# Channel attention on one core: the row buffer starts 128 bytes earlier in SBUF

## The chip, the core and the metric

The kernel runs on one core of a Trainium2 chip. Its time is the device time of one execution in microseconds (us). Before the change it is 717.7 us, the median of 3 runs (717.59 to 718.36).

## What is computed

The input x is an image of 384 x 384 places with 384 channels in bf16, 113.25 MB. The mean of every channel over all places is multiplied by one weight (the kernel size k is 1, so the convolution over channels is a product), goes through a sigmoid, and scales its channel:

```
g = jnp.einsum("bhwc->bc", x) / (H * W)
s = sigmoid(g * w1d[0])            # the loop over k, with k = 1
return x * s[:, None, None, :]
```

All of x must have been read before the first output can be written, and x is larger than the core's on-chip memory (SBUF).

## The kernel before, in words

**Rows and partitions.** One row is the 384 channels of one place, 768 bytes. The 147,456 rows are spread over 128 partitions, 1,152 each. The first chunk of the image, 785 rows for each partition, is called STREAMED; the second, 367 rows for each partition, KEPT. A partition's rows of a chunk lie next to each other in HBM, so a transfer of n rows is, in each partition, one run of n x 768 bytes in HBM and one run in SBUF.

**The arena.** Nearly all of SBUF is one tile, `arena`, with 275 rows for each partition (211,200 bytes of it). Every load and every store of the image goes into or out of it; TensorE, VectorE, ScalarE and GpSimd read it, the last three write it. The tiles of the pool are laid out in the order of their declarations, each rounded up to a multiple of 32 bytes for each partition.

**First half, about 268 us.** SyncE's queue loads rows (`load`, L235, its DMA at L240). TensorE sums them with a matrix of ones into one PSUM bank (`sum_rows`, L257, its instructions recorded at L246). STREAMED rows are summed and overwritten. KEPT rows remain: VectorE folds four rows into the room of three (`fold`, L296, with the helpers at L280 and L286; ScalarE checks at L317 that the dropped exponent bits are the expected ones and leaves its findings in `seen`). Some rows are copied to the PSUM banks as well (L382). The table `PLAN` (L396) sets the order of loads, sums and folds.

**The turn.** ScalarE takes the sigmoid of the sums (L431), with the factor `w_sc` as its scale. `w_sc` comes from the weight, which was loaded to `w_bf`.

**Second half.** VectorE, and GpSimd beside it, multiply rows by the result (`scale`, L439, recorded at L444); VectorE unfolds the folded rows first (L491 on). SyncE's queue stores the rows (`store`, L465, its DMA at L471) and loads the 784 rows of STREAMED that are no longer there a second time. A loop (L724 on), run when the program is written, keeps a model of the DMA queue and so fixes the order of all these steps; nothing in it depends on addresses in SBUF. At the end `worst` (the largest entry of `seen`), `odd` and `odd_i` tell GpSimd whether any row had unexpected exponents, in which case rows would be done again; with this data none has.

**Waits.** `Flow` (L107 and L113 among its lines) writes each step out on its engine with the semaphores it needs. All of the image's transfers are on SyncE's one queue, in one order.

Of the kernel before, what the change touches and what calls it, by code (L numbers as in the profile page):

```python
# [131 lines left out]
def kernel(  # L132
# [12 lines left out]
    P = nc.NUM_PARTITIONS  # L145
    B, H, W, C = x.shape
# [5 lines left out]
    bf16, f32, u16, u32 = x.dtype, mybir.dt.float32, mybir.dt.uint16, mybir.dt.uint32  # L152
# [15 lines left out]
    ROWS = Y + 2 * PIECE  # L168
# [13 lines left out]
    pool = ctx.enter_context(tc.tile_pool(name="sb", bufs=1))  # L182
# [2 lines left out]
    pieces = [(g, lo, min(PIECE, q - lo)) for g, (_, q) in enumerate(GROUPS) for lo in range(0, q, PIECE)]  # L185

    ones = pool.tile([P, P], bf16, name="ones")
    w_bf = pool.tile([1, 1], bf16, name="w_bf")
    w_sc = pool.tile([P, 1], f32, name="w_sc")
    worst = pool.tile([P, 1], f32, name="worst")  # L190
    odd = pool.tile([P, 1], bf16, name="odd")
    arena = pool.tile([P, ROWS, C], bf16, name="arena")
    s_bf = pool.tile([P, C], bf16, name="s_bf")
    rest = pool.tile([P, P], bf16, name="rest")
    seen = pool.tile([P, 2 * len(pieces)], f32, name="seen")
# [664 lines left out]
```

## Time and profile before

| | |
|---|---|
| median of the runs | 717.7 us |
| the profiled execution | 717.85 us |
| its span, from the first to the last instruction | 715.6 us |
| transfers of the image on SyncE's queue | 63 loads, 48 stores |
| read from HBM, written | 190.32 MB, 113.25 MB |
| busiest engine | VectorE (DVE), 467.5 us |

The profile's page names the engines PE (TensorE), DVE (VectorE), ACT (ScalarE), POOL (GpSimd) and SP (SyncE); SPq is SyncE's queue. A group's row has the line in the kernel, the engine, the operation, output and input tile, shapes and count, then the busy time in us, the mean of one in ns, and the idle time before it with what ended it. A stage's row has the stretch and its length in us, then each engine's busy time with its count of instructions, the clock granted to TensorE, the share of the 16 DMA engines' time that their packets fill, and the rate in GB/s. A queue's row has packets, MB, and the share of the 16 engines' time. A packet is what one DMA engine moves as one piece: here one partition's run of one transfer, or a few bytes that report its end.

### The profile page before, as it was taken

What the parts mean: (1) busy time and instruction counts of PE and PEld (TensorE: products, weight loads), DVE (VectorE), ACT (ScalarE), POOL (GpSimd) and SP (SyncE); (2) the same over time, 40 slices, a digit from 0 to 9 for tenths busy, and PEclk for the clock granted to TensorE, in tenths of its full rate; (3) what the DMA queues carried; (4) which work ended last, traced back from release to release, by engine and by line L of the source; (5) the groups of instructions that cost most, each with busy time, mean ns of one, the idle gap of its engine ahead of it and who ended that gap; (6) DMA issues with size and microseconds to landing.
All of it is one profiled execution on the core that took longest, in us unless ns stands there. A gap on an engine that the chain in (4) does not pass through costs nothing.

```text
span 715.6 us, 2106 instructions
## 1 busy us (share of the span) xinstructions
PE 221.1 (31%) x1279; PEld 0.3 (0%) x3; DVE 467.5 (65%) x383; ACT 116.5 (16%) x97; POOL 98.0 (14%) x46
## 2 busy tenths in 40 slices
PE   4658877999998890000000000000000000000000
PEld 0000000000000000000000000000000000000000
DVE  4600001898989849999999999999940597007840
ACT  3700001576667630000110000000000000000000
POOL 0000000000000005414233431167100000000000
PEclk9899989999999996555555555555555555555555
DMA  9999999999999989999999999999999999999997
GB/s 382 428 446 419 439 431 425 447 422 433 425 430 427 430 351 379 407 418 435 427 428 437 441 422 437 443 435 430 444 414 459 423 431 442 420 435 439 442 426 326
DMA packets 15997, 303.70 MB, mean 424 GB/s; under 512 B 1778, under 2 KB 2418, under 8 KB 5106
## 3 DMA queue, kind: packets, MB, share of 16 engines
q1 hardware_dynamic: 15984, 303.57, 99.0%
q8 instruction: 5, 0.08, 0.0%
q14 instruction: 6, 0.05, 0.0%
q10 hardware_dynamic: 2, 0.00, 0.0%
HBM read 190.32 MB, written 113.25 MB: 424 GB/s over the span
## 4 chain that ended last, share of the span: by engine, by line
DMA 49%; DVE 29%; PE 16%; ACT 1%; issue 1%; DVEq 0%; SPq 0%; another core or an unknown queue 0%; POOLq 0%
DMA arena<-in_x_dram 37%; DVE arena L444 20%; PE bank L246 16%; DMA out_dram<-arena 11%; DVE arena L280 5%; DVE arena L286 4%; ACT arena L317 1%; DVEq L107 0%; SPq L471 0%; SPq L240 0%; ACT s_bf L431 0%; SPq L113 0%; SPq L855 0%; POOLq L107 0%
## 5 line engine op out<-in xcount | busy, mean ns | idle before, releaser
L246 PE MATMUL bank<-arena,ones 128*128 128x384 bf16 x1151 | 200.6, 337 | 37.5 <-DMA arena<-in_x_dram 37.5
L280 DVE TENSOR_SCALAR arena<-arena 128x1536 uint16<-128x1536 uint16 (+2 forms) x199 | 140.5, 751 | 107.1 <-DMA arena<-in_x_dram 100.0
L444 POOL TENSOR_TENSOR arena<-arena,s_bf 128x768 bf16<-128x768 bf16 (+3 forms) x42 | 97.8, 2333 | 426.5 <-ACT bank L435 268.1
L444 DVE TENSOR_TENSOR arena<-arena,bank 128x3072 bf16<-128x3072 bf16 (+13 forms) x61 | 138.0, 2303 | 4.4 <-DMA arena<-in_x_dram 3.7
L444 DVE TENSOR_TENSOR arena<-arena,s_bf 128x5376 bf16<-128x5376 bf16 (+4 forms) x27 | 76.5, 2902 | 94.9 <-DMA arena<-in_x_dram 84.8
L317 ACT ACTIVATE arena<-arena 128x3072 uint16<-128x3072 uint16 (+1 forms) x38 | 102.5, 2696 | 146.2 <-DVE arena L280 146.2
L286 DVE TENSOR_TENSOR arena<-arena 128x3072 uint16<-128x3072 uint16 (+2 forms) x90 | 117.7, 1307 | 12.2 <-PE bank L246 9.3
L561 PE MATMUL bank<-odd,ones 128*128 128x1 bf16 x1 | 0.2, 187 | 259.5 <-DVE odd L556 259.5
L246 PE MATMUL bank<-s_bf,ones 128*128 128x384 bf16 x125 | 22.1, 326 | 0.0
L382 ACT COPY arena<-bank 128x512 uint32<-128x512 uint32 (+2 forms) x8 | 4.2, 533 | 87.4 <-DMA out_dram<-arena 87.3
L317 ACT ACTIVATION_READ_ACCUMULATOR arena<-arena 128x1 f32 x38 | 7.1, 187 | 0.0
L382 ACT COPY bank<-arena 128x512 uint32<-128x512 uint32 (+2 forms) x8 | 3.8, 527 | 0.0
L260 PE MATMUL bank<-arena,ones 128*128 128x384 bf16 x1 | 0.5, 479 | 6.9 <-DMA arena<-in_x_dram 6.9
L431 ACT ACTIVATE s_bf<-bank,w_sc 128x384 bf16<-128x384 f32 x1 | 0.6, 580 | 9.4 <-PE bank L246 9.4
L828 ACT ACT_TABLE_LOAD x1 | 1.3, 1283 | 0.7 <-PEq L844 0.7
L337 DVE MEMSET ones<- 128x128 bf16 x1 | 0.2, 165 | 1.1 <-PEq L844 1.1
L342 PE MATMUL bank<-w_bf,ones 1*128 1x1 bf16 x1 | 0.2, 182 | 2.1 <-DMA w_bf<-in_w1d_dram 2.1
L347 DVE TENSOR_SCALAR w_sc<-bank 128x1 f32<-128x1 f32 x1 | 0.2, 159 | 0.9 <-PE bank L342 0.9
L565 DVE CAST odd_i<-bank 128x1 int32<-128x1 f32 x1 | 0.2, 157 | 0.3 <-PE bank L561 0.3
L561 PEld LDWEIGHTS bank<-odd,ones 128*128 128x128 bf16 x1 | 0.1, 105 | 517.6 <-DVE odd L556 517.6
L435 ACT COPY bank<-s_bf 128x192 uint32<-128x192 uint32 x1 | 0.3, 323 | 0.0
L382 ACT COPY arena<-rest 128x64 uint32<-128x64 uint32 x1 | 0.2, 244 | 0.0
(10 smaller groups left out, 1.4 us busy)
## 6 DMA issues: line engine op xcount, KB each, us to landing
arena<-in_x_dram SPq DMA_DIRECT2D x3, 6912.0 KB, 36.2
out_dram<-arena SPq DMA_DIRECT2D x3, 6912.0 KB, 28.4
arena<-in_x_dram SPq DMA_DIRECT2D x4, 4608.0 KB, 24.2
arena<-in_x_dram SPq DMA_DIRECT2D x6, 3072.0 KB, 19.8
out_dram<-arena SPq DMA_DIRECT2D x6, 3072.0 KB, 21.5
arena<-in_x_dram SPq DMA_DIRECT2D x2, 6144.0 KB, 30.7
arena<-in_x_dram SPq DMA_DIRECT2D x2, 4992.0 KB, 23.4
arena<-in_x_dram SPq DMA_DIRECT2D x1, 8160.0 KB, 26.5
```

Source lines behind the costliest of these rows:

```text
L246: return pe.add_instruction(mybir.InstMatmult(name=nc.get_next_instruction_name(), ins=[pe.lower_ap(rhs), pe.lower_ap(ones[:])], outs=[pe. ...
L260: return nc.tensor.matmul(acc, lhsT=ones[:], rhs=arena[:, i, :], start=first, stop=last)
L280: lambda: nc.vector.tensor_scalar(out=dst, in0=src, scalar1=s0, scalar2=s1, op0=op0, op1=op1),
L286: "DVE", lambda: nc.vector.tensor_tensor(out=dst, in0=a, in1=b, op=op), reads=reads, writes=writes
L317: lambda: nc.scalar.activation(out=y, in_=y, func=ACTF.Copy, accum_out=seen[:, 2 * k + i : 2 * k + i + 1]),
L337: fl.add("DVE", lambda: nc.vector.memset(ones[:], 1.0), writes=["ones"])
L382: "ACT", lambda: nc.scalar.copy(dst.bitcast(u32), src.bitcast(u32)), reads=reads, writes=writes
L431: lambda: nc.scalar.activation(out=s_bf[:], in_=acc, func=ACTF.Sigmoid, scale=w_sc[:, 0:1]),
L435: "ACT", lambda: nc.scalar.copy(s_ps.bitcast(u32), s_bf[:].bitcast(u32)), reads=["s_bf"], writes=["bank0"]
L444: lambda: vec.tensor_tensor(out=v, in0=v, in1=s[:, None, :].to_broadcast([P, n, C]), op=Op.mult),
L561: lambda: nc.tensor.matmul(votes, lhsT=ones[:], rhs=odd[:], start=True, stop=True),
L828: nc.scalar.preload_act_table(ACTF.Sigmoid)
```

## The change

The four small tiles `w_bf`, `w_sc`, `worst` and `odd` are declared behind the arena and no longer in front of it. Each takes 32 bytes of a partition. The pool begins at byte 16,512 of a partition with `ones`, 256 bytes.

| tile | first byte before | first byte after |
|---|---|---|
| `ones` | 16,512 | 16,512 |
| the four small tiles | 16,768 to 16,864 | 227,968 to 228,064 |
| `arena` | 16,896 = 66 x 256 | 16,768 = 65.5 x 256 |
| `s_bf` | 228,096 | 228,096 |

```diff
     ones = pool.tile([P, P], bf16, name="ones")
+    arena = pool.tile([P, ROWS, C], bf16, name="arena")
     w_bf = pool.tile([1, 1], bf16, name="w_bf")
     w_sc = pool.tile([P, 1], f32, name="w_sc")
     worst = pool.tile([P, 1], f32, name="worst")
     odd = pool.tile([P, 1], bf16, name="odd")
-    arena = pool.tile([P, ROWS, C], bf16, name="arena")
     s_bf = pool.tile([P, C], bf16, name="s_bf")
```

Every engine has the same instructions in the same order before and after, SyncE's transfers included. The lines of the kernel keep their numbers, apart from those of the five declarations.

## The prediction

> **What bounds the kernel now.** I read the page's totals first, then the stages, then the DMA queue's own packets.
>
> ```profile
> span 715.6 us, 2106 instructions
> PE 221.1 (31%) x1279; PEld 0.3 (0%) x3; DVE 467.5 (65%) x383; ACT 116.5 (16%) x97; POOL 98.0 (14%) x46
> DMA packets 15997, 303.70 MB, mean 424 GB/s; under 512 B 1778, under 2 KB 2418, under 8 KB 5106
> q1 hardware_dynamic: 15984, 303.57, 99.0%
> HBM read 190.32 MB, written 113.25 MB: 424 GB/s over the span
> ```
>
> No engine is busy for more than 65% of the span, but the packets of queue q1 fill 99.0% of the time of 16 DMA engines. The chain of waits names three parties, and it would mislead a reader who stopped there:
>
> ```profile
> DMA 49%; DVE 29%; PE 16%; ACT 1%; issue 1%; DVEq 0%; SPq 0%; another core or an unknown queue 0%; POOLq 0%
> ```
>
> It follows dependencies. A PE or DVE piece on it runs while the DMA engines still have earlier transfers queued. The table by stage shows this; its last two columns are the DMA share (1.00 means all 16 engines busy) and GB/s:
>
> ```profile
> 0.00:20.00 20.00, 8.89 (x42) 0.20 (x2) 10.17 (x18) 8.57 (x7) 0.20 (x4) 1.00 0.95 393
> 20.00:110.00 90.00, 64.76 (x352) 0.00 (x0) 9.42 (x16) 11.17 (x15) 0.00 (x0) 0.91 1.00 431
> 110.00:215.00 105.00, 99.84 (x600) 0.00 (x0) 79.83 (x109) 60.88 (x43) 0.00 (x0) 0.98 1.00 431
> 215.00:265.00 50.00, 44.96 (x272) 0.00 (x0) 39.17 (x53) 30.54 (x22) 0.00 (x0) 1.00 1.01 425
> 265.00:290.00 25.00, 2.46 (x16) 0.00 (x0) 21.71 (x18) 0.90 (x2) 9.21 (x3) 0.65 0.86 335
> 290.00:350.00 60.00, 0.00 (x0) 0.00 (x0) 57.36 (x33) 0.00 (x0) 21.49 (x10) 0.50 1.01 424
> 350.00:450.00 100.00, 0.00 (x0) 0.00 (x0) 97.34 (x64) 4.41 (x9) 35.03 (x12) 0.50 1.01 433
> 450.00:550.00 100.00, 0.19 (x1) 0.10 (x1) 76.33 (x53) 0.00 (x0) 32.12 (x18) 0.50 1.01 436
> 550.00:640.00 90.00, 0.00 (x0) 0.00 (x0) 39.27 (x13) 0.00 (x0) 0.00 (x0) 0.50 1.00 432
> 640.00:715.60 75.60, 0.00 (x0) 0.00 (x0) 36.87 (x13) 0.00 (x0) 0.00 (x0) 0.50 0.95 410
> ```
>
> Outside the start, the turn from reading to writing (265 to 290) and the tail, the DMA share is 1.00 or 1.01 (a packet that crosses a window's edge counts whole). So what is added to the packets is added to the time; where the engines idle, about 1.0 us at the start, 25 x 0.14 = 3.5 us at the turn and 75.6 x 0.05 = 3.8 us at the end, the idling is for the first bytes, the sigmoid and the last landing, which stay.
>
> **What a packet costs now.** A rate and a fixed price come out of two stretches that hold only loads, one of large packets and one of small:
>
> ```profile
> DMA packets 907, 38.77 MB, mean 431 GB/s; under 512 B 101, under 2 KB 101, under 8 KB 101
> q1 hardware_dynamic: 906, 38.76, 99.6%
> ...
> DMA packets 2650, 21.27 MB, mean 425 GB/s; under 512 B 294, under 2 KB 425, under 8 KB 1277
> q1 hardware_dynamic: 2648, 21.24, 100.5%
> ```
>
> The first pair is 20 to 110 us: 906 packets and 38.76 MB took 99.6% of 16 x 90 us = 1,434.2 us. The second is 215 to 265 us: 2,648 packets and 21.24 MB took 100.5% of 16 x 50 us = 804.0 us. With f for each packet and b for each MB, 906f + 38.76b = 1,434.2 and 2,648f + 21.24b = 804.0. Scaling the first by 21.24/38.76 and subtracting leaves 2,151f = 18.1 us, so f = 8.4 ns (about 0.5 ns either way from the rounding of the shares) and b = 36.81 us, which is 27.17 GB/s for one engine. Over the whole span this gives (15,984 x 0.0084 + 303.57 x 36.81)/16 = 706.8 us, where the page's 99.0% is 708.4: nothing large is missing. All 16 engines reach 434.7 GB/s, and the stages stand at 431 to 436.
>
> **The change part by part.** The order of instructions on every engine, and the size and shape of each, stay as they are, so nothing is removed, added or moved past a queue. Four tiles of 32 bytes come to stand behind the arena. The arena's first byte goes from 16,896 = 66 x 256 to 16,768 = 65.5 x 256, and since a row is 768 = 3 x 256 bytes, every row then starts 128 bytes past a multiple of 256. The tiles from s_bf on keep their addresses. The four small tiles are used by seven instructions in all; I cost these at nothing wherever the tiles lie. They run beside the full DMA queue; without that cover even a doubling of the longest of them would add 0.6 us:
>
> ```profile
> L431 ACT ACTIVATE s_bf<-bank,w_sc 128x384 bf16<-128x384 f32 x1 | 0.6, 580 | 9.4 <-PE bank L246 9.4
> L347 DVE TENSOR_SCALAR w_sc<-bank 128x1 f32<-128x1 f32 x1 | 0.2, 159 | 0.9 <-PE bank L342 0.9
> ```
>
> What is left is the arena's side of every transfer. Their number:
>
> ```profile
> L240 SPq DMA_DIRECT2D arena<-in_x_dram x63: 327/339/1270, 0.9 to 622.4; - x63
> L471 SPq DMA_DIRECT2D out_dram<-arena x48: 332/333/1268, 268.5 to 688.3; - x48
> ```
>
> 63 loads and 48 stores are 111 transfers of 128 partitions. Each sends one data packet per partition: 111 x 128 = 14,208, and with 16 small ones per transfer 111 x 144 = 15,984, the count of q1 exactly. One engine thus carries 888 data packets, 504 of loads and 384 of stores.
>
> The trace has no packet whose SBUF side starts off a multiple of 256, so the price is bounded. From below: nothing, if only the number of bytes counts. A gain would have to come out of the 8.4 ns, and I see no reason why a start off a boundary should shorten them. From above, within one packet: if SBUF is read and written in blocks of 256 bytes, a packet of n blocks that starts in the middle of one touches n + 1, a whole block more, 256 x 36.81e-6 us = 9.4 ns; this is close to paying the fixed price a second time. I take half of that, 128 bytes or 4.7 ns: the half block ahead of the first byte is carried for nothing, while the last block can stop at its last byte. It is the middle of the bounds, and the nearest row, the 8.4 ns, doesn't exclude either end.
>
> 888 x 4.7 ns = 4.2 us. The profiled execution took 717.85 us (715.6 of span and 2.25 around it), which becomes 722.0; the median of the runs shown, 717.7, is 0.15 lower, so I predict **721.9 us**, slower by 0.6%. Nothing is subtracted for cover: the 15 stores at the turn carry 120 packets an engine, so at most 0.6 us could vanish there. If it is on loads alone, 504 x 4.7 = 2.4 us gives 720.1; on stores alone, 384 x 4.7 = 1.8 us gives 719.5; at a whole block, 888 x 9.4 = 8.4 us gives 726.1. These are the forecast's own range, 719.5 to 726.1.
>
> The Trainium skill's page "DMA: Bandwidth & Descriptors" (How a descriptor splits into AXI transactions) says that a transaction must start at a multiple of 256 bytes, so that a descriptor which doesn't start there begins at the boundary below it and the bytes ahead of its start still cost time. It speaks of reading; SBUF is read by the stores alone, and by that reading the sum would be the 719.5 above. No row here shows it, since every row starts at a multiple of 256.
>
> **The rivals.**
>
> *The half block is hidden* (not slower). Each packet already has 8.4 ns in which no byte flows at the engine's rate. If the side that touches SBUF can fetch or drain ahead in that pause, 4.7 ns more fit into it, at every packet, and nothing comes out: 717.7 us. It decides as long as the extra is below 8.4 ns and the pause belongs to the other side of the engine. For it: transfers in this trace already start at odd multiples of 256 on the HBM side in every second partition (the two chunks hold 785 and 367 rows of 768 bytes per partition, both odd), so their two sides differ modulo 512, and the stages still run at 431 to 436 GB/s. Against it: none of these starts is off a multiple of 256.
>
> *Each block is cut.* If the two sides of a transfer must agree modulo 256, each 256 bytes would be handled in two pieces, and the price falls on 303.57 MB/256/16 = 74,100 blocks per engine instead of 888 packets. At an eighth of a block's time, 1.18 ns, that is 87 us: 805 us (772 with loads alone, 190.32 MB; 750 with stores alone, 113.25 MB). At the whole fixed price of 8.4 ns it would be 622 us more. It outgrows the forecast from 0.06 ns a block on. For it speaks only that the rates stand at one same ceiling, so that any loss shows in full; against it, that the difference modulo 512 costs nothing now.
>
> *The engines feel it.* DVE is busy for 57.36 + 97.34 us of the 160 from 290 to 450. Were its operations on the arena 2% longer, 3.1 us would appear there, and the stores that wait for them would be late: 720.8 us. Against it: each operation runs over whole rows, thousands of bytes per partition, and its start is a small part of it.
>
> *Faster.* The chain's PE and DVE parts have no reason to shorten; a gain over 0.2% would be a shorter packet, by 1.6 ns at least, 716.3 us or less.
>
> **How the numbers follow.** Forecast 0.40, hidden 0.34, cut blocks 0.17, engines 0.04, faster 0.05. A measurement here can tell about 0.2%, 1.4 us. Of the forecast's case 0.02 falls below that bound (part of the stores' half block covered), so faster 0.05, same 0.34 + 0.02 = 0.36, slower 0.38 + 0.17 + 0.04 = 0.59. The range runs from 716.8, the hidden case with scatter (the runs shown spread over 0.8 us), to 726.5, the whole block with as much: it holds forecast, hidden and engines, 0.78, and a little of faster, and leaves the cut blocks out.
>
> **What would show it.** In the changed kernel the two load-only stretches, solved as above, should give b = 36.8 us per MB again and f = 13.1 ns instead of 8.4, with the same 15,984 packets. If f stays at 8.4 and the span at 715.6, the half block is hidden. If b grows, the blocks are cut, and the GB/s in the stages fall below 425. If both stay and DVE's mean durations at L444 grow, it is the engines. A rise in the stores' stages (550 to 640 and the tail) alone would put the price on reading SBUF. I am wrong if the time leaves 719.5 to 726.1.

## The result, and the profile after

The changed kernel takes 722.33 us (median of 4 runs, 721.73 to 722.62) against 717.9 us before: a ratio of 1.006, 95% interval 1.0047 to 1.0073. Run again as experiment e9 it came to 721.68 us, 1.0051 (1.0034 to 1.0068). It is slower by some 4 us, and the predicted 721.9 us was met. The profile shows that it was met for a partly wrong reason.

The page of the changed kernel, in the lines that answer to those of before:

```profile
span 720.2 us, 2106 instructions
PE 223.0 (31%) x1279; PEld 0.3 (0%) x3; DVE 467.7 (65%) x383; ACT 116.5 (16%) x97; POOL 98.2 (14%) x46
DMA packets 15997, 303.70 MB, mean 422 GB/s; under 512 B 1778, under 2 KB 2418, under 8 KB 5106
q1 hardware_dynamic: 15984, 303.57, 98.8%
DMA 56%; DVE 22%; PE 16%; ACT 1%; issue 1%; DVEq 0%; SPq 0%; another core or an unknown queue 0%; POOLq 0%
```

The packets and bytes are the same, and so is the engines' work: DVE 467.7 us against 467.5, ACT 116.5 both times. The span is 4.6 us longer, with the DMA queue still full: by the sum of their records its packets take 711.5 us (98.8% of 720.2), where they took 708.6 (99.0% of 715.6). So about 3 us are longer packets and the rest is time without one.

The stages of the changed kernel from 20 us on, to be read against the prediction's table (the last two columns are DMA share and GB/s):

```profile
20.00:110.00 90.00, 64.76 (x352) 0.00 (x0) 9.40 (x16) 11.17 (x15) 0.00 (x0) 0.89 1.00 431
110.00:215.00 105.00, 100.19 (x597) 0.00 (x0) 79.40 (x108) 60.49 (x43) 0.00 (x0) 0.97 1.00 429
215.00:265.00 50.00, 44.40 (x269) 0.00 (x0) 39.59 (x53) 30.96 (x22) 0.00 (x0) 1.00 1.01 422
265.00:290.00 25.00, 3.69 (x22) 0.00 (x0) 20.49 (x18) 0.91 (x2) 9.22 (x3) 0.62 0.85 323
290.00:350.00 60.00, 0.00 (x0) 0.00 (x0) 57.83 (x32) 0.00 (x0) 21.50 (x10) 0.50 1.00 421
350.00:450.00 100.00, 0.00 (x0) 0.00 (x0) 95.34 (x63) 4.41 (x9) 33.38 (x11) 0.50 1.01 431
450.00:550.00 100.00, 0.18 (x1) 0.10 (x1) 79.28 (x54) 0.00 (x0) 33.90 (x18) 0.50 1.01 434
550.00:640.00 90.00, 0.00 (x0) 0.00 (x0) 39.27 (x13) 0.00 (x0) 0.00 (x0) 0.50 1.00 433
640.00:720.20 80.20, 0.00 (x0) 0.00 (x0) 36.87 (x13) 0.00 (x0) 0.00 (x0) 0.50 0.93 402
```

The small loads of 215 to 265 us run at 422 GB/s, before at 425, with the DMA share at 1.01 in both. Between 290 and 550 us the rates are 2 to 3 GB/s lower too, but these windows are fixed in time while the program runs over 1 us late, so they don't hold the same transfers. The large transfers of 550 to 640 us run at 433, before at 432. The tail has a share of 0.93, before 0.95.

The prediction's sign that engines feel the new address, a longer mean at L444, isn't there. The first line is before, the second the changed kernel:

```profile
L444 DVE TENSOR_TENSOR arena<-arena,bank 128x7680 bf16<-128x7680 bf16 x10 | 41.4, 4149 | 0.8 <-DMA arena<-in_x_dram 0.8
L444 DVE TENSOR_TENSOR arena<-arena,bank 128x7680 bf16<-128x7680 bf16 x10 | 41.4, 4148 | 1.3 <-DMA arena<-in_x_dram 1.3
```

The two load-only stretches (20 to 110 and 215 to 265 us) of the changed kernel, to be solved as the prediction did:

```profile
q1 hardware_dynamic: 910, 38.81, 99.8%
...
q1 hardware_dynamic: 2440, 21.06, 100.5%
```

910f + 38.81b = 1,437.1 and 2,440f + 21.06b = 804.0 give 1,946f = 24.2 us: f = 12.4 ns, where it was 8.4, and b = 36.74 us per MB, where it was 36.81. The predicted f was 13.1 with b unchanged. As far as this test goes, the prediction holds. The rate of 422 GB/s in the small loads is below the 425 that it named as a sign of cut blocks, but b did not grow.

The single packets say more. For each data packet, the table takes its time less its bytes at 27.2 GB/s and less 8.2 ns (close to the 27.17 and 8.4 of the prediction's fit): what is left is an extra. Short ones (under 30 ns) and stalls (30 ns and over) are summed apart and divided by 16 engines; "none" is the span less the time of all packets.

```
us of the span      short extras           stalls                      none   span
                    to 267  267-300  on    to 60  60-300  300-450  on
before               0.07    0.13   0.01    0.74   1.29    0.56   0.02   6.95  715.6
changed              1.10    0.66   0.05    0.71   1.50    0.90   0.74   8.68  720.2
changed again, e9    1.05    0.66   0.03    0.78   1.60    0.58   0.78   8.52  719.8
```

Of the 4.6 us, 1.6 are short extras, 1.2 stalls and 1.7 time without a packet. Nearly all short extras are in two places: 1.10 us in the 43 loads of the first half, and 0.66 us in the 15 small stores at the turn. From 300 us on, the stalls aside, loads and stores alike cost what they did: the median store of 55,296 bytes takes 2,041 ns in both kernels, and the median load of that size too. The half block on every packet isn't there.

The stores at the turn pay as much as the loads. Their 13 of 1,536 to 9,984 bytes have a mean short extra of 4.6 ns, before 0.2 (the two of 768 bytes are left out, as one of them is lengthened by 14 ns before as well). They pay although the queue was empty ahead of them, from 267.8 to 270.6 us. The stores of 7,680 to 9,984 bytes that follow from 300 us on pay nothing.

### The profile page after: what moved, and what is told of

The parts are those of the page before. It is cut to its first block, busy times and chain, and to the rows that moved or that the text cites. A ratio compares the mean times of both kernels' runs of the same rounds, so it can differ in the third digit from the quotient of the medians.

```text
span 720.2 us, 2106 instructions
## 1 busy us (share of the span) xinstructions
PE 223.0 (31%) x1279; PEld 0.3 (0%) x3; DVE 467.7 (65%) x383; ACT 116.5 (16%) x97; POOL 98.2 (14%) x46
## 3 DMA queue, kind: packets, MB, share of 16 engines
q1 hardware_dynamic: 15984, 303.57, 98.8%
## 4 chain that ended last, share of the span: by engine, by line
DMA 56%; DVE 22%; PE 16%; ACT 1%; issue 1%; DVEq 0%; SPq 0%; another core or an unknown queue 0%; POOLq 0%
DMA arena<-in_x_dram 42%; DVE arena L444 17%; PE bank L246 16%; DMA out_dram<-arena 14%; DVE arena L280 3%; DVE arena L286 2%; ACT arena L317 1%; DVEq L107 0%; SPq L471 0%; SPq L240 0%; ACT s_bf L431 0%; SPq L113 0%; SPq L855 0%; POOLq L107 0%
## 5 line engine op out<-in xcount | busy, mean ns | idle before, releaser
L246 PE MATMUL bank<-arena,ones 128*128 128x384 bf16 x1151 | 202.7, 339 | 36.8 <-DMA arena<-in_x_dram 36.7
L444 POOL TENSOR_TENSOR arena<-arena,s_bf 128x768 bf16<-128x768 bf16 (+3 forms) x42 | 98.0, 2336 | 430.2 <-ACT bank L435 269.3
L444 DVE TENSOR_TENSOR arena<-arena,bank 128x3072 bf16<-128x3072 bf16 (+13 forms) x61 | 138.1, 2304 | 6.8 <-DMA arena<-in_x_dram 6.3
L444 DVE TENSOR_TENSOR arena<-arena,s_bf 128x5376 bf16<-128x5376 bf16 (+4 forms) x27 | 76.5, 2901 | 96.0 <-DMA arena<-in_x_dram 85.6
L260 PE MATMUL bank<-arena,ones 128*128 128x384 bf16 x1 | 0.5, 477 | 6.9 <-DMA arena<-in_x_dram 6.9
L431 ACT ACTIVATE s_bf<-bank,w_sc 128x384 bf16<-128x384 f32 x1 | 0.6, 582 | 9.7 <-PE bank L246 9.7
## 6 DMA issues: line engine op xcount, KB each, us to landing
arena<-in_x_dram SPq DMA_DIRECT2D x4, 4608.0 KB, 24.2
```

The costliest lines, as they stand in the source:

```text
L246: return pe.add_instruction(mybir.InstMatmult(name=nc.get_next_instruction_name(), ins=[pe.lower_ap(rhs), pe.lower_ap(ones[:])], outs=[pe. ...
L260: return nc.tensor.matmul(acc, lhsT=ones[:], rhs=arena[:, i, :], start=first, stop=last)
L431: lambda: nc.scalar.activation(out=s_bf[:], in_=acc, func=ACTF.Sigmoid, scale=w_sc[:, 0:1]),
L444: lambda: vec.tensor_tensor(out=v, in0=v, in1=s[:, None, :].to_broadcast([P, n, C]), op=Op.mult),
```

## The experiments

**Other offsets: e1, e2, e10.** The whole kernel, with the arena at other addresses; only the order of the declarations differs. For e1 (64 bytes past a multiple of 256) and e10 (32 bytes past):

```diff
 # e1
     ones = pool.tile([P, P], bf16, name="ones")
+    seen = pool.tile([P, 2 * len(pieces)], f32, name="seen")
     w_bf = pool.tile([1, 1], bf16, name="w_bf")
+    arena = pool.tile([P, ROWS, C], bf16, name="arena")
     w_sc = pool.tile([P, 1], f32, name="w_sc")
...
 # e10
     odd = pool.tile([P, 1], bf16, name="odd")
+    odd_i = pool.tile([P, 1], mybir.dt.int32, name="odd_i")
     arena = pool.tile([P, ROWS, C], bf16, name="arena")
```

For e2, `rest` (256 bytes) comes in front of the arena instead, so that it starts at an odd multiple of 256.

> The arena starts 64 bytes past a multiple of 256 (byte 16,960). Theory A, the prediction's: each packet carries the bytes of its first block that lie ahead of its start, here 64 instead of 128, so half the extra: about 2.1 us, 720 us, and in the load-only stretches f about 10.7 ns. Theory B, any start off a multiple of 256 costs the same, because one more block is touched whatever the offset: about 4.4 us, 722.3 us, f about 12.4 ns. Theory C, only starts off a multiple of 128 or 256 in some other way disturb the order in which engines take turns: no number from the bytes; more than 4.4 us is then as possible as less.

> The arena starts at an odd multiple of 256 (byte 17,152 = 67 x 256); before, at an even one (66 x 256). All theories that go by 256 expect the time of before, 717.9 us, and f = 8.4 ns. If what counts is any difference of the start to before, or a multiple of 512, it comes out above 719.3 us.

> The arena starts 32 bytes past a multiple of 256 (byte 16,928). If a packet paid for the bytes ahead of its start: a quarter of the change's price, 1 ns a load packet, about 718.9 us. If any start off a multiple of 256 costs the same, as 64 and 128 bytes seem to: 4 ns a load packet, 721.4 to 722.4 us. If 32 bytes, less than 64, adds a cost of its own: above 723 us.

Measured: e1 721.43 us, 1.0056 (1.0039 to 1.0073); e10 722.16 us, 1.0062 (1.0045 to 1.0079); e2 717.72 us, 1.0002 (0.9993 to 1.0012). Over 110 to 260 us the mean short extra of a load packet was 0.18 ns before, 0.13 in e2, 3.87 in the changed kernel, 3.91 in e1 and 4.86 in e10. For the 13 small stores at the turn it was 0.2 ns before and in e2, 4.6 in the changed kernel, 4.1 in e1 and 3.9 in e10. So of the offsets tried, only the multiples of 256 are free, an odd one as much as an even one, and the price of a load doesn't shrink with the bytes ahead of the start: 32 of them cost no less than 128. That is theory B of e1 and not A. It rules out the prediction's price (the bytes before the start, carried for nothing) even where packets do get longer.

**Transfers alone: e3 and e4.** Every instruction but SyncE's is left out, at both addresses:

```diff
+        if eng not in ('SP',):
+            return None
         s = Step(eng, emit, dma)
...
-        deps = set(after)
+        deps = {d for d in after if d}
```

> The kernel before with every instruction of TensorE, VectorE, ScalarE and GpSimd left out, so nothing is summed, scaled, folded or checked and the output is the unscaled input where rows were not overlaid; the same 111 transfers stay in the same order on the same queue, and wait only for one another. All theories: the packets' own sum, (15,984 x 0.0084 + 303.57 x 36.81)/16 = 706.8 us, plus the start and the tail, 711 to 715 us.

> As e3_dma_only_0 (the same instructions left out), with the arena 128 bytes past a multiple of 256. Theory A, the extra belongs to the packet alone: all packets, loads and stores, 4.2 us above e3. Theory D, it belongs to the packet, but only to loads (SBUF written): 504 packets an engine x 4 ns = 2.0 us above e3. Theory E, it comes from the meeting of the transfers with engines that read and write the arena (TensorE and ScalarE are busy in the first half alone, where the longer packets of the changed kernel stand): within 0.5 us of e3.

e3 took 714.36 us, 0.9951 of the kernel before (0.9934 to 0.9967), e4 717.74 us, 0.9998 (0.9988 to 1.0008): 3.4 us apart. e3 lies in the 711 to 715 that were expected. Theory E falls, since hardly an engine ran: the stages of e4 list ACT, POOL, TensorE's clock, DMA share and GB/s, and no other engine appears.

```profile
0.00:20.00 20.00, 1.28 (x1) 0.20 (x4) 1.00 0.95 393
20.00:110.00 90.00, 0.00 (x0) 0.00 (x0) 1.00 0.99 430
110.00:215.00 105.00, 0.00 (x0) 0.00 (x0) 1.00 1.00 431
215.00:260.00 45.00, 0.00 (x0) 0.00 (x0) 1.00 1.01 424
```

The same stages of e3:

```profile
20.00:110.00 90.00, 0.00 (x0) 0.00 (x0) 1.00 1.00 433
110.00:215.00 105.00, 0.00 (x0) 0.00 (x0) 1.00 1.00 431
215.00:260.00 45.00, 0.00 (x0) 0.00 (x0) 1.00 1.00 427
```

Theories A (4.2 us) and D (2.0 us) both miss the 3.4, and the packets of e4 show why: the extra, 4.04 ns over 110 to 260 us, is in loads, as D says, but not in those of the second half (0.14 ns from 300 to 440 us, loads and stores together). The small stores at the turn have it too, 5.0 ns against 0.0 in e3. Of the 3.0 us between the two profiled spans, 1.7 are short extras, 0.6 stalls and 0.7 time without a packet. The extra isn't there at the beginning either. The share of packets that are lengthened by over 2 ns, by stretches of 20 us:

```
from us   0   20   40   60   80  100  120  140  160  180  200  220  240
e3      .12  .10  .10  .03  .05  .00  .00  .00  .00  .00  .00  .00  .00
e4      .11  .12  .13  .27  .36  .47  .72  .68  .70  .69  .64  .65  .63
before  .11  .05  .11  .02  .04  .09  .06  .01  .03  .00  .00  .00  .00
changed .11  .05  .17  .46  .55  .50  .66  .62  .64  .67  .66  .59  .61
```

Both arenas begin with some lengthened packets. At a multiple of 256 they die out, in e3 by 100 us; at 128 past it they multiply until about two thirds of all packets are lengthened, nearly all of these by 2 to 12 ns. That led to theory F: a state that builds up in a run of loads.

**A long run of loads, then a long run of stores: e5 and e6.** On e4 and e3, the second half is replaced:

```diff
+    for i in range(39):
+        load(STREAMED, 20 * (i % 13), 20 * i, 20 * i + 20)
+    load(STREAMED, 260, 780, 784)
+    for chunk, rows_of in ((STREAMED, N_STREAM + 1), (KEPT, N_KEPT - 1)):
+        for i, lo in enumerate(range(0, rows_of, 24)):
+            store(chunk, 24 * (i % 11), lo, min(lo + 24, rows_of))
```

> Transfers alone, arena 128 bytes past a multiple of 256. The first half's 43 loads as they are, then 40 loads (39 of 20 rows) without a store between them, then all 1,152 rows of each partition stored in 49 stores (what is stored is whatever lies in the arena, unscaled). Theory F, the longer packets are a state that builds up in a run of loads and ends where the transfers turn from stores back to loads: the extra of about 4 ns a packet lasts through all 450 us of loads, and the stores begin with it. Theory G, it belongs to the first half of the kernel (its addresses, the number of transfers queued): it ends with the 43 loads at about 265 us. Theory H, stores pay as well, in a long run of them: extra of some ns through the last 260 us; if stores are free, it fades there.

> As e5_long_128 with the arena at a multiple of 256. All theories: no extra beyond 0.5 ns a packet on average in the stretches of one direction, and with F and a share of stores about 320 loads an engine more that pay, e5 lies some 2.7 to 4 us above this one.

e5 took 712.70 us, 0.9931 (0.9909 to 0.9954), e6 710.22 us, 0.9893 (0.9865 to 0.9922): 2.5 us apart, a little under the 2.7 that was the low end. The queue's packets of e5, first in the loads of 300 to 440 us, then in the stores of 480 to 700 us:

```profile
q1 hardware_dynamic: 4381, 59.92, 100.7%
...
q1 hardware_dynamic: 5832, 94.99, 100.6%
```

The same of e6:

```profile
q1 hardware_dynamic: 4428, 60.40, 100.8%
...
q1 hardware_dynamic: 5843, 94.92, 100.5%
```

With the bytes at the 36.81 us per MB of before, the loads of e5 leave 2,255.7 - 2,205.7 = 50.0 us for 4,381 packets, 11.4 ns each, those of e6 2,257.9 - 2,223.3 = 34.6 us for 4,428, 7.8 ns. For the stores it is 7.6 ns in e5 and 7.5 in e6. So the loads paid 3.6 ns a packet up to 170 us beyond the place where the kernel turns to storing (4.16 against 0.10 ns by the packets' records), as F expects and G doesn't. In the long run of stores nothing is paid: of the packets from 451 us on, none is lengthened by over 2 ns in e5 or e6, and a store of 18,432 bytes takes a mean of 686.0 ns in both. H falls, and so does the prediction's price on every one of 384 store packets an engine. The first store behind the loads of e5 still has a share of .22, the next one .00; the small stores at the turn of the whole kernel, which pay, are stores of another kind, and why they do for some 18 us stays open.

The Trainium skill's page "DMA: Bandwidth & Descriptors" (How a descriptor splits into AXI transactions) has a read that starts off a multiple of 256 bytes pay for the bytes down to the boundary. Stores are what reads SBUF here, and the 7.6 and 7.5 ns of the long run don't show such a price: either it is hidden in that fixed time, or it isn't paid. The small stores at the turn do pay, but 4.6, 4.1 and 3.9 ns for 128, 64 and 32 bytes, which isn't in proportion to those bytes. What the runs show besides, a price on loads, which write SBUF, the section doesn't state.

**What ends it: e7 and e8.** On e4, two stores of one row each among the loads of the first half (e7; the second of them stands before the 21st load, not the 20th as expected below), or two pauses in which the queue waits for all earlier transfers (e8). A further line of e7, which makes the later stores wait for these two, isn't shown:

```diff
 # e7, in load
+        at = len(fl.steps)
+        if at in (12, 21):
+            i = 92 if at == 12 else 68
+            fl.add(
+                "SP",
+                lambda: nc.sync.dma_start(out=view(of, *STREAMED)[:, at : at + 1, :], in_=arena[:, i : i + 1, :]),
+                reads=rows(i, 1), writes=["out"], dma=True,
+            )
...
 # e8, in load
             writes=rows(a, hi - lo), dma=True,
+            after=list(fl.steps) if len(fl.steps) in (12, 20) else (),
```

> e4_dma_only_128 with two stores of one row put into the first half, before the 13th and the 20th load (about 133 and 198 us). Theory F: after each, the share of lengthened load packets falls from 0.6 or 0.7 to under 0.2 and climbs again over some 50 us. If turning is not what ends it: the share stays at 0.6 to 0.75 from 120 us on, as in e4.

> e4_dma_only_128 with two pauses in the first half: the 13th and the 21st transfer wait until all earlier ones have landed, about 2 us without a packet each. If what ends the state is that all engines stop and start together: the share of lengthened packets falls to under 0.2 behind each pause, as F expects of a turn. If it takes a store, the share stays at 0.6 to 0.75 behind the pauses.

e7 took 718.75 us, 1.0009 (0.9998 to 1.0021), e8 723.19 us, 1.0071 (1.0048 to 1.0094); e8's pauses cost far more than they saved: 0.3 us of short extras in the 43 loads, while e8 took 5.4 us longer than e4. Share of lengthened packets, by transfer:

```
e7: load, KB per partition     24   one-row store     39    24    36    24
    starts at us            128.0           135.3  135.6 147.3 154.6 165.6
    share over 2 ns           .70             .02    .10   .63   .70   .71
e8: load, KB per partition     24           pause     39    24    36    24    29    24    18
    starts at us            128.2                  137.5 149.8 157.0 167.9 175.2 184.1 191.3
    share over 2 ns           .66                    .15   .00   .00   .01   .12   .61   .70
e8, second pause: load, KB per partition     24    15     6    14     9    15     9
    starts at us                          205.0 212.8 217.4 219.2 223.6 226.3 230.9
    share over 2 ns                         .28   .00   .00   .00   .09   .48   .58
```

The pause wipes the state out, though the first load behind each has 19 or 21 stalls from the restart. Behind the first pause the loads are clean for some 40 us, and at 184 us they are where they were; behind the second they are clean for only some 20 us. Counted in loads the two agree: five, or 40 packets an engine, before the share is back near .5 or above. That hints at a number of packets and not a time, but two pauses don't show it, and the empty queue ahead of the stores at the turn didn't spare them. A turn also wipes it out (.70 to .10, and .70 to .09 at the second one), but only for the one load behind it, not for the 50 us that F expected. F is right that the state builds up and is ended by a turn, and wrong on how long a turn lasts.

**The changed kernel again: e9.**

> The changed kernel once more, for what one execution can't tell apart: of its 4.6 us of span, 2.8 are packets and 1.3 stand in the tail, after 700 us. If the uneven finish of the 16 engines belongs to the change, the idle time of the tail is again 1 us or more above the 3.4 of before; if it is chance, it lies anywhere between 2.9 and 5.4, as in the other shifted kernels. Load packets of 110 to 260 us again about 4 ns longer, stores of 300 us on not longer.

Its rows are in the table of the first section: loads 3.86 ns longer over 110 to 260 us, and stalls behind 450 us of 0.78 us, as in the first profile. Time without a packet after 700 us was 4.8 us; it was 4.9 in the changed kernel and in e10, but 3.1 in e1, with 3.5 before and 3.2 in e2. So in three of four shifted executions of the whole kernel the end is 1.3 to 1.4 us later than the packets explain, and in the fourth it isn't: over its whole span, e1 has only 0.3 us more without a packet than before, where the changed kernel has 1.7. That this part belongs to the change is likely, and not shown.

## Why the prediction was right, and where it was wrong

- **What bounds the kernel** held: whatever lengthened the packets came out in the time, with the engines' own work unchanged. With the engines left out, 3.4 us remained of the 4.4 of the first measurement, or of the 3.9 of e9; the remaining 0.5 to 1.0 us is not explained.
- **The four small tiles cost nothing**: nothing in the runs speaks against it; e2, with the same small tiles in front and another one beside them, is at 717.72. The prediction has all seven instructions beside a full queue, which isn't so for its longest: the sigmoid (L431, at 267.5 us) stands between the last load packet, which ends at 266.7, and the first store packet at 269.4. It took 0.59 us before and after the change, so the term stays nothing.
- **The bounds** (nothing and 9.4 ns a packet) held the measured mean of 4 ns, though single packets pay up to 12. A price per packet, not one per 256 bytes, is also right where one is paid: e4's loads of 9,216 and of 24,576 bytes, from 110 us on, paid 4 to 6 and about 4 ns, and b came out at 36.74 in the changed kernel, so that the cut blocks with their 87 us are out.
- **The step that failed** is the one that took "128 bytes or 4.7 ns: the half block ahead of the first byte is carried for nothing" for all 888 packets of an engine. A long run of stores pays nothing (7.6 against 7.5 ns), the transfers from 300 us on hardly anything, and offsets of 32 and 64 bytes cost about what 128 do. What pays are the 43 loads of the first half, 344 packets an engine, from about 50 us on: 1.0 us, and the 15 small stores at the turn, 120 packets an engine: 0.5 us. The term of 4.2 us thus measured 1.6. The variants "on loads alone", 2.4 us, and "on stores alone", 1.8 us, missed as well.
- **What made up the sum in its place**: 1.2 us more of stalls and 1.7 us more without a packet, neither of which the prediction had. The stalls behind 450 us were 0.01 to 0.02 us in before, e2 and e3 and 0.59 to 0.78 in the changed kernel, e9, e1, e10 and e4. In the changed kernel 0.70 of its 0.74 us stand in two loads right before a turn to stores (49,152 and 36,096 bytes), in packets lengthened by hundreds of ns. The agreement of 4.2 and 4.4 us is thus largely luck.
- **Hidden**, the rival at 717.7, is what the long run of stores and the second half's packets look like; it failed on the loads of the first half and the stores behind them. **The engines feel it** is out by e3 and e4.
- The test that the prediction set itself, f at 13.1 ns, would have confirmed it wrongly (12.4), because both stretches lie in the first half. Its other test, the stage of 550 to 640 us by itself, showed no rise, and that was the one that told the readings apart.

## What to carry to other kernels

In a kernel that is bound by its transfers, place the large tile at a multiple of 256 bytes of a partition: here it is worth 0.5 to 0.6%, for a reordering of declarations. It matters for long unbroken runs of loads and for small stores right behind them; in a long run of stores the offset was free. A forecast that fits a total should be tested on a part in which the rival reading says something else.

## What the runs showed of the hardware that was not expected

- The lengthened packets are a state and not a property of a packet. At a multiple of 256 bytes a disturbance dies out (share .12 at the start, .00 from 100 us in e3); 128 bytes past it, it grows within 60 to 120 us to about .65 and stays (e5, until the loads end at about 445 us); 64 and 32 bytes past it, it grows sooner and reached .88 and .95. Nothing but transfers is needed. What a packet meets when it is lengthened wasn't tried, and stays open.
- It is ended by a pause of the queue for some 40 us in one case and 20 in the other, five loads each time, and by a single one-row store for the 8 packets an engine that follow. Yet the small stores at the turn have it right behind an empty queue. Why they do, and why the long loads of the second half stay clean (0.14 ns in e4 over 300 to 440 us) for longer than that, is open.
- Without disturbance the packets are remarkably exact: 7.5 to 8.4 ns each and 27.2 GB/s an engine, the same within that for loads and stores; and an odd multiple of 256 is as clean as an even one (0.13 against 0.18 ns).
